# A fused attention and two-layer expert kernel: batch 0 grouped, its TensorE and ScalarE order pinned, weight conversions and softmax steps moved to other slots

## The chip, the cores and the metric

The kernel runs on one core of one Trainium2 chip. The metric is the device time of one execution in microseconds; the number compared is the median over runs. The engines are named as in the profile: PE is TensorE's matmul (PEld its weight loads), DVE is VectorE, ACT is ScalarE, POOL is GpSimd, and SP is the queue that issues all DMA transfers.

## The reference

Three layers stand behind one another. Everything is float32.

```python
# 1. Nystrom attention, batch 8, heads 8, S = 576, D = 64, m = 32 landmarks (means over 18 rows)
A  = softmax(scale * q    @ k_lm.T)      # 576 x 32
Bm = softmax(scale * q_lm @ k_lm.T)      #  32 x 32
C  = softmax(scale * q_lm @ k.T)         #  32 x 576
Z  = Bm.T / (norm1(Bm) * norm_inf(Bm) + 1e-6)
for _ in range(6): Z = 2 * Z - Z @ Bm @ Z
x = A @ Z @ C @ v                        # 4608 tokens x 512 after the heads are joined
# 2. gated layer, width 1536
x = (silu(x @ w_gate) * (x @ w_val)) @ w_out
# 3. soft mixture of 8 experts with 4 slots each
logits = x @ phi                         # 4608 x 32
d = softmax(logits, over the tokens); c = softmax(logits, over the slots)
slot_in = d.T @ x                        # 32 x 512
out = c @ expert_ffn(slot_in)            # relu(s @ w1[e]) @ w2[e]
```

## The kernel before

The attention result is never formed. Per batch b the right-hand factor Z C v is multiplied into the gate and value weights, so that one chunk j of 128 of the 1536 columns needs only the softmaxed scores A (tiles `EH` and `EL`, a high and a low part) times a small matrix G (tiles `GH`, `GL`). The program has three stages.

**The head** (first 40 us). `first_attention` (L361) does the attention of batch 0 alone: landmark sums, scores, softmax and a Newton chain (`m_n`, `m_T`, tile `newton`), and ends with the block `WB`. Pieces of weight conversion are put between its steps (`side`).

**The batches.** For each of 8 batches, `unit` (L948) runs 12 chunks. A chunk has two halves of 288 tokens; a half has six matmuls into a PSUM tile `pg` (gate), an eviction to `u` by ACT (Silu), six matmuls into `pv` (value) and a product `hT` by DVE. After each of these four groups comes a slot, so a batch has 48 slots, n = 4j + i, and the function `slot` puts all other work there by the table `SCHED`:

- `g_product` (L740) multiplies `WB` into the weights: eight matmuls into two PSUM tiles `g`, for one chunk (256 columns) or for a pair of chunks (512 columns); `paired` (L737) decides. ACT then writes `GH`, and DVE subtracts to get `GL` one slot later. Before, batch 0 is never paired.
- `logits` (tile `l`) and `transposes` (into `HB`) of the chunk before.
- `attention(b + 1)` and `a_softmax(b + 1)` (lists `at1`, `at2`, `at3`, `am1` to `am3`; numbers are slots counted from the start of the batch before): landmark sums by DVE (L333), scores `m_a` and `m_c`, exponentials by ACT, the transposes `m_t`, and six Newton steps `m_n` (L670).
- `softmoe(b - 1)` (lists `sm`, `sm1`): softmax of the logits of the batch before, `DN`, an exchange of `DN` between partitions (twelve small DMA transfers, or four matmuls `m_dr` in batch 7), 72 matmuls `m_d` into four PSUM tiles, and their addition to `Sacc` (L921).
- In batch 0 only: the conversion of the weights from float64 storage (lists `w`, `o`: one ACT pass, L176, and for each 512 columns two DVE operations, L192 and L193), and for each chunk the product of `w_out` and phi (list `p`: four transposes `m_wt`, four products `m_p`, one sum `m_ps`, each followed by an ACT copy).

PSUM tiles come from pools by tag: `x` has three buffers (g, m_a, m_c, m_t, m_n, m_d, m_wt, m_p, m_ps), `pg` and `pv` two each, `l` one. A matmul that needs a buffer waits until the engine that evicts the tile from it is done.

**The tail** (last 84 us) loads the expert weights, runs the experts and writes the output.

What sets the order: each engine runs its instructions in one order. From batch 1 on, `keep_order` (L73) pins PE to the order in which the code is written. In the head and in batch 0 the framework's scheduler may reorder the instructions of an engine. Inside SP's queue transfers are issued strictly one after the other, and one that waits for its buffer holds up those behind it. Silu and Exp need different tables in ACT; a change of table is an `ACT_TABLE_LOAD`.

Of the kernel before, what the change touches and what calls it, by code (L numbers as in the profile page):

```python
# [8 lines left out]
F32 = mybir.dt.float32  # L9
# [18 lines left out]
SCHED = {  # L28
# [22 lines left out]
}  # L51
# [3 lines left out]
def nystrom_softmoe_kernel(  # L55
# [488 lines left out]
    def attention(b):  # L544
        assert b == 1 or ("q", b - 1) in seq
        ks, qs = landmark_tiles()
        for nm, dst in (("k", ks), ("q", qs)):
            for hp in range(4):
                (landmark_pool if b == 1 and S_["lp"][2 * hp + (nm == "q")] else landmark)(nm, b, hp, dst)
                if hp == 3 and b > 1:  # L550
                    load_four("q" if nm == "k" else "k", b)
                yield
        def score_tiles(name):
            ms = [psp.tile([128, 512], F32, tag="pv" if i == 3 else "x", name=name, bufs=2 if i == 3 else 3)
                  for i in (3, 0, 1, 2)]
            return {(1, 1): ms[0], (0, 0): ms[1], (0, 1): ms[2], (1, 0): ms[3]}
# [22 lines left out]
        for name, product, eviction in (  # L579
                ("m_a", lambda half, ms: scores(ms, ks, "q", b, half, range(4)), a_eviction),  # L580
                ("m_c", c_product, c_eviction)):
            if together:
                t = score_tiles(name)
                for half in (1, 0):
                    product(half, [t[half, 0], t[half, 1]])
                for half, r in ((1, 1), (0, 0), (0, 1), (1, 0)):
                    eviction(half, r, t[half, r])
                    yield
            else:
                for half in range(2):  # L590
                    ms = [psp.tile([128, 512], F32, tag="x", name=name, bufs=3) for r in range(2)]
                    product(half, ms)
                    for r in range(2):
                        eviction(half, r, ms[r])
                        yield
        if b == 1:
            e_tiles(b)
# [71 lines left out]
        for k in range(6):  # L669
            m = psp.tile([128, 512], F32, tag="x", name="m_n", bufs=3)  # L670
            for q in range(2):
# [65 lines left out]
    def paired(b, j):  # L737
        return 0 < b < nb - 1 and not (b == nb - 2 and j >= NJ - 2)

# [208 lines left out]
    def unit(b, j, slot):  # L948
# [3 lines left out]
        for half in range(2):  # L952
            pg = psp.tile([128, 512], F32, tag="pg", name="pg", bufs=2)
            mm3(pg, b, j, 0, half)
            u = mp.tile([128, HALF], F32, tag="u", name="u", bufs=2)
            by_tanh = 0 < b < nb - 1 and (j, half) in TANH[b > 1]
            if by_tanh:
# [22 lines left out]

    TANH = [{(5, 0), (5, 1), (6, 0)}, {(1, 1), (2, 0), (2, 1)}]
    GROUPS = [2, 2, 4, 8, 8, 8, 4]
# [33 lines left out]

    first_attention(side)
    load_w(5)
    for f in side_pre:
# [67 lines left out]
    for a in range(1, nb):  # L1087
        att, asm = attention(a), a_softmax(a)
        for gen, nm in ((att, "at"), (asm, "am")):
            for r in S_[nm + str(min(a, 3))]:  # L1090
                todo[48 * (a - 1) + r].append(gen)
        sm = softmoe(a - 1)
        for r in S_["sm1" if a == 1 else "sm"]:
            todo[48 * a + r].append(sm)
    prev = None
    n_ins = lambda: len(nc.cur_bb.bb.instructions)
    for b in range(nb):
        if b == 1:
            middle = n_ins()
        for j in range(NJ):  # L1100
            p = prev
            def slot(i):
# [24 lines left out]
                if not first:  # L1127
                    for gen in todo[48 * b + n]:
                        next(gen, None)
                if n == (46 if b == 0 else 45) and b + 1 < nb:  # L1130
                    g_unit(b + 1, 0)
                if n == (47 if b == 0 else 46):
                    g_low()
# [211 lines left out]
```

## Time and profile before

| what | value |
|---|---|
| median of 3 runs | 676.5 us (674.85 to 676.81) |
| the profiled execution | 674.4 us, its span 672.6 us |
[...]
| PE busy | 623.9 us, 93% of the span |
| DVE, ACT, POOL busy | 478.0, 298.8, 73.3 us |
| batches 0 to 7 begin at | 40.4, 125.9, 200.3, 266.2, 332.1, 398.0, 463.9, 527.7 us |
| the last pv matmul ends at | 588.4 us |

The profiled execution lies 2.1 us under the median of the runs. A batch begins here with its first pg matmul. Matmuls overlap, so a busy PE is not a PE at its peak; the difference between a stretch and its busy time is idle time. In rows of stretches each row has its bounds and length in us, the busy time and number of instructions of each engine, and at its end the granted TensorE clock, the busy share of the DMA engines and the GB/s that they moved.

### The profile page before, as it was taken

Reading aid. Unit: us, or ns where it says so; the run is one execution under the profiler, and the core shown is the slowest. Engines: PE = TensorE matmul, PEld = TensorE weight load, DVE = VectorE, ACT = ScalarE, POOL = GpSimd, SP = SyncE. Lnnn points to the kernel's source line nnn. Section 1 sums busy time; section 2 is a strip of 40 time slices with the busy share of each in tenths; the row PEclk is TensorE's granted clock in tenths of the full one; section 3 lists DMA queues with packets and bytes.
Section 4 is the critical chain, followed back from the end, with each engine's and each line's share of the span. In section 5 each row is a group of like instructions: output and inputs, shape, how many; then the busy total and the mean of one; then the engine's idle time right before and its main releaser. Section 6 shows DMA issues by size and latency. Waiting matters only on the chain. (4 is left out here: it accounts for less than half of the span.)

```text
span 672.6 us, 18315 instructions
## 1 busy us (share of the span) xinstructions
PE 623.9 (93%) x7591; PEld 465.8 (69%) x7591; DVE 478.0 (71%) x1154; ACT 298.8 (44%) x764; POOL 73.3 (11%) x81
## 2 busy tenths in 40 slices
PE   5699999998999999999999999999999999989991
PEld 2575667784877877787787778777778777843560
DVE  4999989878578777868785978597856645550441
ACT  2566875445438323732383338233823442320441
POOL 0400012013011101110111012001300000010000
PEclk9799999998999999999999999999999999999996
DMA  8788773233222222222222222122120595699999
GB/s 281 271 322 331 269 280 129 87 113 116 73 72 83 75 72 73 84 75 73 72 86 73 71 87 76 69 71 72 57 86 2 160 378 184 220 288 348 348 369 337
DMA packets 63299, 106.47 MB, mean 158 GB/s; under 512 B 4977, under 2 KB 33009, under 8 KB 61681
## 3 DMA queue, kind: packets, MB, share of 16 engines
q1 hardware_dynamic: 63216, 105.32, 47.1%
q8 instruction: 59, 0.97, 0.6%
q14 instruction: 24, 0.19, 0.1%
HBM read 91.24 MB, written 12.58 MB: 154 GB/s over the span
## 5 line engine op out<-in xcount | busy, mean ns | idle before, releaser
L312 ACT ACTIVATE u<-pg 128x288 f32<-128x288 f32 x174 | 71.9, 413 | 138.4 <-PE pg L945 130.8
L974 DVE TENSOR_TENSOR hT<-u,pv 128x288 f32<-128x288 f32 x174 | 77.7, 447 | 40.1 <-PE pv L945 36.3
L945 PE MATMUL pg<-EH,GH 128*128 128x288 f32 x384 | 93.9, 324 | 2.6 <-ACT GH L765 1.6
L779 DVE TENSOR_TENSOR GL<-g,GH 128x512 fp32r<-128x512 f32 (+1 forms) x122 | 66.4, 572 | 37.7 <-ACT GH L765 37.6
L945 PE MATMUL pg<-EH,GL 128*128 128x288 f32 x384 | 85.7, 299 | 1.7 <-DVE GL L779 1.5
L945 PE MATMUL pv<-EH,GH 128*128 128x288 f32 x384 | 84.0, 298 | 0.0
L945 PE MATMUL pg<-EL,GH 128*128 128x288 f32 x384 | 83.5, 296 | 0.0
L945 PE MATMUL pv<-EL,GH 128*128 128x288 f32 x384 | 82.6, 296 | 0.0
L945 PE MATMUL pv<-EH,GL 128*128 128x288 f32 x384 | 82.2, 295 | 0.0
L765 ACT CAST GH<-g 128x512 fp32r<-128x512 f32 (+1 forms) x122 | 54.2, 495 | 55.0 <-PE g L748 54.9
L945 PEld LDWEIGHTS pg<-EH,GH 128*128 128x128 f32 x384 | 60.0, 189 | 22.8 <-issue 15.5
L799 DVE STREAM_TRANSPOSE HB<-hT 128x576 f32<-128x576 f32 x96 | 74.3, 774 | 1.8
L945 PEld LDWEIGHTS pg<-EH,GL 128*128 128x128 f32 x384 | 62.2, 188 | 4.7 <-DVE GL L779 3.8
L945 PEld LDWEIGHTS pv<-EH,GH 128*128 128x128 f32 x384 | 61.6, 188 | 2.6 <-issue 1.2
L945 PEld LDWEIGHTS pg<-EL,GH 128*128 128x128 f32 x384 | 61.8, 188 | 0.9 <-issue 0.9
L945 PEld LDWEIGHTS pv<-EL,GH 128*128 128x128 f32 x384 | 61.5, 188 | 0.9 <-issue 0.9
L945 PEld LDWEIGHTS pv<-EH,GL 128*128 128x128 f32 x384 | 61.6, 188 | 0.5 <-issue 0.5
L748 PE MATMUL g<-w,WB 64*32 64x512 f32 (+1 forms) x976 | 56.4, 510 | 0.4 <-ACT WB L535 0.4
L794 PE MATMUL l<-hT,P_sb 128*32 128x160 f32 (+1 forms) x768 | 45.2, 298 | 0.8 <-DVE hT L974 0.6
L794 PEld LDWEIGHTS l<-hT,P_sb 128*32 128x32 f32 x768 | 15.2, 108 | 39.8 <-DVE hT L974 16.5
L913 PE MATMUL m_d<-HB,HB 32*32 32x384 f32 x864 | 38.4, 514 | 2.6 <-DMA HB<-DN 2.3
L913 PE MATMUL m_d<-HB,DN 32*32 32x384 f32 x288 | 37.7, 514 | 0.0
(248 smaller groups left out, 946.4 us busy)
## 6 DMA issues: line engine op xcount, KB each, us to landing
k<-in_kT_dram SPq DMA_DIRECT2D x52, 288.0 KB, 3.7
ffn<-in_w_dram SPq DMA_DIRECT2D x13, 1024.0 KB, 9.0
ffn<-in_w_dram SPq DMA_DIRECT2D x24, 512.0 KB, 9.0
HB<-in_w_cat_dram SPq DMA_DIRECT2D x8, 1024.0 KB, 8.0
v<-in_v_dram SPq DMA_DIRECT2D x8, 1024.0 KB, 5.8
q<-in_qT_dram SPq DMA_DIRECT2D x28, 288.0 KB, 3.0
HB<-in_w_out_dram SPq DMA_DIRECT2D x12, 512.0 KB, 5.8
wr<-in_w_cat_dram SPq DMA_DIRECT2D x4, 1024.0 KB, 8.7
```

Of the source, the lines that this page charges most:

```text
L312: i = act.activation(*a, **kw)
L748: pe.matmul(gs[r][32 * hp:32 * hp + 32, 0:256 * n].rearrange("p (u f) -> p u f", u=n), WB[b % 2][64 * r:64 * r + 64, hp, :], w[64 * r:64 * ...
L765: act.copy(H_, g)
L779: dve.tensor_tensor(out=GL, in0=g, in1=GH, op=ALU.subtract)
L794: pe.matmul(L[32 * c:32 * c + 32, 0:32 * k], P_sb[:, j, :], main[:, 0:k, c, :], start=j == 0, stop=j == NJ - 1)
L799: dve.transpose(HB[b % 2][:, S * j:S * j + S].rearrange("p (t r) -> p t r", r=32), hT[:, 0:S].rearrange("p (t r) -> p t r", r=32))
L913: pe.matmul(ms[a][32 * g:32 * g + 32, 0:384].rearrange("p (j f) -> p j f", j=NJ), d_of(a, g, k), hb[32 * a:32 * a + 32, :, 4 * k + g, :], ...
L945: pe.matmul(ps[:, 0:HALF], G_t[b, j, q, sel_][h], e[:, q, ts_], start=n == 0, stop=n == 5)
L974: dve.tensor_tensor(out=o, in0=u, in1=pv[:, 0:HALF], op=ALU.mult)
```

## The change

The core of the diff; of the tables only the lines that are spoken of stand here, and `w`, `o`, `p`, `at1`, `am1`, `at2`, `am2` get new slot numbers throughout.

```diff
-    'loads': ['w1', 'q0', 'o0', 'w0', 'v0', 'o1', 'q1', 'v1', 'w2', 'w4', 'p', 'w3'],
+    'loads': ['w1', 'q0', 'o0', 'w0', 'v0', 'o1', 'q1', 'w2', 'w3', 'w4', 'p', 'v1'],
...
-    'sm1': [1, 2, 4, 19, 20, 21, 24, 25, 25, 28],
+    'sm1': [1, 2, 4, 13, 15, 16, 25, 26, 26, 28],
+    'sm7': [1, 2, 3, 6, 10, 15, 23, 24, 24, 28],
...
-    'u0': [1, 3, 3, 0],
+    'u0': [1, 1, 1, 0],
...
-    'lw': [0, 0, 0, 0, 0, 0, 0, 0, 0, 0, 0, 0],
+    'lw': [0, 0, 0, 0, 0, 1, 0, 1, 0, 1, 0, 1],
...
@@ attention(b): the landmark sums of q come behind the scores m_a for b == 1
+        yield from landmarks("k", ks)
+        if b > 1:
+            yield from landmarks("q", qs)
...
+                if name == "m_a":
+                    yield from landmarks("q", qs)
@@ the Newton steps
-            m = psp.tile([128, 512], F32, tag="x", name="m_n", bufs=3)
+            m = psp.tile([128, 512], F32, tag="pg", name="m_n", bufs=2)
@@
     def paired(b, j):
-        return 0 < b < nb - 1 and not (b == nb - 2 and j >= NJ - 2)
+        return (b > 0 or j >= 4) and b < nb - 1 and not (b == nb - 2 and j >= NJ - 2)
@@ unit
-            by_tanh = 0 < b < nb - 1 and (j, half) in TANH[b > 1]
+            by_tanh = b < nb - 1 and (j, half) in TANH[min(b, 2)]
@@
-    TANH = [{(5, 0), (5, 1), (6, 0)}, {(1, 1), (2, 0), (2, 1)}]
+    TANH = [{(4, 1), (5, 0), (5, 1)}, {(3, 1), (4, 0), (4, 1)}, {(1, 1), (2, 0), (2, 1)}]
@@
     first_attention(side)
+    in_order("silu", warm, one, AF.Silu)
@@ the lists of generators for each slot
+    for a in range(1, nb):
         sm = softmoe(a - 1)
-        for r in S_["sm1" if a == 1 else "sm"]:
+        for r in S_["sm1" if a == 1 else "sm7" if a == nb - 1 else "sm"]:
             todo[48 * a + r].append(sm)
@@
+    middle = n_ins()
     for b in range(nb):
         if b == 1:
-            middle = n_ins()
+            keep_order(mybir.EngineType.Activation, middle, n_ins())
```

So in batch 0 chunks 4 to 11 get their G in pairs; PE's order is pinned from batch 0 on and ACT's within batch 0; four of the weight conversions (chunks 5, 7, 9, 11) do their low word with a second ACT pass, and need two DVE operations fewer each; three halves of batch 0 get their Silu from Tanh, which saves a change of table, at one DVE operation each; the Silu table is loaded in the head; the attention of batches 1 and 2 runs some slots earlier; within a slot the steps of all attention generators come ahead of those of `softmoe`; the Newton steps use the PSUM buffers of `pg`.

**PE in batch 0, around the G product of chunks 4 and 5.** Tiles as above (`HB_85` is the work space of the `w_out` product; in the rows of the changed kernel line numbers are 1 to 7 higher). Before, the unit of chunk 5:

```order
L945 MATMUL pg<-EH,GH 128x288
L945 MATMUL pv<-EH,GH 128x288
L945 MATMUL pg<-EH,GH 128x288
L794 MATMUL l<-hT,P_sb 32x160 x2
L794 MATMUL l<-hT,P_sb 32x128 x2
L945 MATMUL pg<-EL,GH 128x288 x2
L945 MATMUL pg<-EH,GL 128x288
L945 MATMUL pv<-EH,GH 128x288
L269 MATMUL m_wt<-cst,HB_85 128x128 x4
L945 MATMUL pg<-EH,GL 128x288
L945 MATMUL pv<-EL,GH 128x288 x2
L945 MATMUL pv<-EH,GL 128x288 x2
```

Now, from the paired G product in the unit of chunk 3 on:

```order
L755 MATMUL g<-w_630,WB_75 32x512 x8
L801 MATMUL l<-hT,P_sb 32x160 x2
L801 MATMUL l<-hT,P_sb 32x128 x2
L279 MATMUL m_p<-HB_85 32x128 x4
L952 MATMUL pg<-EH,GH 128x288 x2
L952 MATMUL pg<-EL,GH 128x288 x2
L952 MATMUL pg<-EH,GL 128x288 x2
L952 MATMUL pv<-EH,GH 128x288 x2
L952 MATMUL pv<-EL,GH 128x288 x2
L952 MATMUL pv<-EH,GL 128x288 x2
L285 MATMUL m_ps<-cst,HB_85 128x32
L270 MATMUL m_wt<-cst,HB_85 128x128 x4
```

The groups of six matmuls stay whole, the other work stands between them, and one G product of 512 columns serves two chunks.

**PE in batch 2, where `softmoe` and the Newton steps meet** (the same in batches 3 to 6). Before, the end of m_d and what follows it:

```order
L913 MATMUL m_d<-HB_85,DN 32x384
L913 MATMUL m_d<-HB_85,HB_84 32x384 x2
L672 MATMUL m_n<-RV,bd 128x96 x2
L945 MATMUL pg<-EH,GH 128x288 x2
L945 MATMUL pg<-EL,GH 128x288 x2
```

Now, the beginning of m_d and what stands ahead of it:

```order
L801 MATMUL l<-hT,P_sb 32x160 x2
L801 MATMUL l<-hT,P_sb 32x128 x2
L679 MATMUL m_n<-RV,bd 128x96 x2
L920 MATMUL m_d<-HB_85,DN 32x384
L920 MATMUL m_d<-HB_85,HB_84 32x384 x4
```

The Newton step moved from behind the m_d matmuls to the place ahead of them.

**ACT in batch 0, at the exponentials of batch 1's attention** (`CE`, `AN` its score tiles; `w_...` a weight conversion, `HB_85<-HB_85` one of `w_out`). Before, its first change of table and the change back:

```order
L312 ACT_TABLE_LOAD
L312 ACTIVATE CE_617,stat<-CE_617,stat 128x576
L176 ACTIVATE HB_85<-HB_85 128x512
L765 CAST GH<-g 128x256 x2
L285 COPY P_sb<-m_ps 128x32
L312 ACTIVATE CE_617,stat<-CE_617,stat 128x32
L312 ACTIVATE CE_618,stat<-CE_618,stat 128x576
L312 ACTIVATE CE_618,stat<-CE_618,stat 128x32
L176 ACTIVATE HB_85<-HB_85 128x512
L312 ACT_TABLE_LOAD
L312 ACTIVATE u<-pg 128x288
```

Now, the only change of table to Exp in batch 0 and what follows it:

```order
L313 ACT_TABLE_LOAD
L313 ACTIVATE CE_533,stat<-CE_533,stat 128x576
L313 ACTIVATE CE_533,stat<-CE_533,stat 128x32
L286 COPY P_sb<-m_ps 128x32
L271 COPY HB_85<-m_wt 128x512
L313 ACTIVATE CE_534,stat<-CE_534,stat 128x576
L313 ACTIVATE CE_534,stat<-CE_534,stat 128x32
L313 ACTIVATE AN_530<-AN_530 128x576
L313 ACTIVATE AN_531<-AN_531 128x576
L966 ACTIVATE u<-pg 128x288
L177 ACTIVATE w_953<-HB_85 128x1024
```

The four exponentials share one table load, and the eviction `u` behind them is a Tanh (L966) and needs no other table.

## Rows read from the trace of the kernel before

**Rows 1.** Batches 0, 1, 3, 7, tail: length; PE, PEld, DVE, ACT, POOL busy (count).
```profile
40.38:125.93 85.55, 81.79 (x931) 60.02 (x930) 78.78 (x182) 59.90 (x141) 8.75 (x7) 1.00 0.72 262
125.93:200.28 74.35, 70.78 (x862) 53.21 (x859) 54.86 (x131) 31.50 (x82) 10.59 (x10) 0.98 0.28 86
266.17:332.08 65.91, 64.80 (x826) 51.01 (x825) 51.78 (x127) 29.06 (x77) 8.45 (x8) 1.00 0.25 77
527.74:588.41 60.67, 58.35 (x714) 45.87 (x712) 33.37 (x75) 21.65 (x57) 0.12 (x1) 1.00 0.78 261
588.41:672.60 84.19, 65.04 (x724) 35.02 (x723) 28.62 (x80) 24.19 (x58) 4.71 (x11) 0.93 1.03 337
```

**Rows 2.** What PE waited for in batch 0: total us, times, longest.
```profile
PE pg L945 <- ACT GH L765: 1.6, 2, 0.9
PE pg L945 <- ACT u L312: 0.9, 1, 0.9
```

**Rows 3.** Batches 0 and 3, tile pg: length; PE, PEld, DVE, ACT busy.
```profile
40.38:125.93 85.55, 29.48 (x144) 20.99 (x144) 0.00 (x0) 9.95 (x24) 1.00 0.72 262
266.17:332.08 65.91, 24.71 (x144) 20.32 (x145) 1.35 (x3) 9.90 (x24) 1.00 0.25 77
```

**Rows 4.** The same stretches, tile pv: length; PE, PEld, DVE busy.
```profile
40.38:125.93 85.55, 26.66 (x144) 20.84 (x144) 10.43 (x24) 1.00 0.72 262
266.17:332.08 65.91, 22.98 (x146) 20.46 (x144) 10.62 (x24) 1.00 0.25 77
```

**Rows 5.** The same stretches, tile g (columns as in rows 3).
```profile
40.38:125.93 85.55, 9.42 (x192) 2.55 (x192) 9.92 (x25) 8.32 (x25) 1.00 0.72 262
266.17:332.08 65.91, 6.53 (x96) 1.09 (x96) 7.97 (x13) 6.42 (x12) 1.00 0.25 77
```

**Rows 6.** Timeline of PE, batch 1: start, us, instruction, idle before and releaser.
```profile
157.07 0.83 PE L913 MATMUL m_d<-HB,DN 32*32 32x384 f32 x2
...
161.87 0.51 PE L913 MATMUL m_d<-HB,HB 32*32 32x384 f32 x2 [2.28 <-DMA HB<-DN]
...
167.56 0.53 PE L945 MATMUL pv<-EH,GH 128*128 128x288 f32 x2
```

**Rows 7.** Timeline of SP, batch 1: the exchange of DN.
```profile
152.77 7.81 SPq L879 DMA_DIRECT2D HB<-DN  x12
```

**Rows 8.** A stretch within batch 1's m_d (columns as in rows 1).
```profile
162.86:166.27 3.41, 3.41 (x84) 2.41 (x92) 2.86 (x5) 0.00 (x0) 1.49 (x2) 0.50 0.45 138
```

**Rows 9.** Timeline of PE, batch 3: the first m_d and the Newton step.
```profile
299.56 0.51 PE L913 MATMUL m_d<-HB,DN 32*32 32x384 f32 x1
...
304.53 0.69 PE L672 MATMUL m_n<-RV,bd 128*128 128x96 f32 x4 [0.65 <-DVE Sacc L923]
```

**Rows 10.** Timeline of PE, batch 7: the exchange by matmuls.
```profile
538.53 0.55 PE L882 MATMUL m_dr<-DN,cst 32*128 32x160 f32 x6 [1.92 <-DVE DN L867]
```

**Rows 11.** DVE in batch 0, groups: shapes, count, busy us, mean ns, idle before.
```profile
L974 DVE TENSOR_TENSOR hT<-u,pv 128x288 f32<-128x288 f32 x24 | 10.7, 447 | 2.2 <-PE pv L945 1.7 <-ACT u L312 0.6
L192 DVE TENSOR_SCALAR w<-w 128x512 int32<-128x512 int32 x20 | 10.0, 522 | 0.5 <-ACT w L176 0.3
L779 DVE TENSOR_TENSOR GL<-g,GH 128x256 fp32r<-128x256 f32 x24 | 9.2, 416 | 0.5 <-ACT GH L765 0.5
L333 DVE TENSOR_REDUCE qs<-q 128x32 f32<-128x576 f32 x4 | 2.9, 741 | 0.0
```

**Rows 12.** ACT in batch 0, groups: table loads and one conversion pass.
```profile
L176 ACT ACTIVATE w<-HB 128x1024 f32<-128x1024 f32 x6 | 6.9, 1147 | 0.0
L312 ACT ACT_TABLE_LOAD x5 | 6.4, 1283 | 0.9 <-DVE stat L608 0.9
```

**Rows 13.** Timeline of ACT in the head: a copy of the Newton chain.
```profile
26.07 0.27 ACT L503 COPY newton<-m_n 128x128 f32<-128x128 f32 x1 [1.00 <-PE m_n L468]
```

**Rows 14.** Timeline of SP in the head: the load of batch 1's v.
```profile
34.71 0.38 SPq L165 DMA_DIRECT2D v<-in_v_dram  x1
```

**Rows 15.** Page, DMA issues: KB each, median us to landing.
```profile
wr<-in_w_cat_dram SPq DMA_DIRECT2D x4, 1024.0 KB, 8.7
```

More of the change, by code (lines that the diff above doesn't have):

```diff
@@ L546, in attention, with landmarks @@
         ks, qs = landmark_tiles()
-        for nm, dst in (("k", ks), ("q", qs)):
+        def landmarks(nm, dst):
             for hp in range(4):
-                (landmark_pool if b == 1 and S_["lp"][2 * hp + (nm == "q")] else landmark)(nm, b, hp, dst)
+                landmark(nm, b, hp, dst)
                 if hp == 3 and b > 1:
@@ L1129, in slot @@
                         next(gen, None)
-                if n == (46 if b == 0 else 45) and b + 1 < nb:
+                if n == 45 and b + 1 < nb:
                     g_unit(b + 1, 0)
-                if n == (47 if b == 0 else 46):
+                if n == 46:
                     g_low()
```

18 rows, old and new, of the table SCHED are left out of this document.

## The prediction

> **What bounds the kernel now.** The first view is the busy time by stretch [rows 1]. In a middle batch TensorE is busy 64.80 of 65.91 us and the vector engine only 51.78, so TensorE is the bound there, with 1.11 us idle. Batch 0 is 85.55 us long, 19.64 longer, and has two engines near their limit: TensorE 81.79 and DVE 78.78. ACT has 59.90. Batch 1 takes 74.35, which is 8.44 above a middle batch. In the tail the DMA share is 1.03 at 337 GB/s with PE busy 65.04 of 84.19: the transfers bound it. Its loads go into space that the work before it sets free, so I count a gain ahead of the tail in full, and come back to that for batch 7.
>
> Then I asked what TensorE waits for in batch 0. The waits over half a microsecond are two on `GH` (1.6 together) and one on `u` (0.9) [rows 2], most of the idle time of 85.55 - 81.79 = 3.76 us. Next the same busy time by tile. The 144 pg matmuls take 29.48 in batch 0 and 24.71 in batch 3 [rows 3], about as many pv matmuls 26.66 and 22.98 [rows 4]: the same work is 4.77 + 3.68 = 8.45 us dearer. The order of before shows why that can be: the scheduler puts other work into the middle of a group of six. The G product takes 9.42 against 6.53 [rows 5].
>
> Then the timelines at the two places where batches 1 and 7 differ from a middle batch. In batch 1 the `m_d` stretch goes from 157.07 to 167.56, 10.49 us, with a wait of 2.28 on the exchange of `DN` in it [rows 6]; the twelve transfers are issued from 152.77 on for 7.81 us [rows 7], so the last landed 161.87 - 152.77 = 9.1 us after the first issue. Behind that wait the granted clock is 0.50 for 3.41 us, although PE is busy in all of them [rows 8]. The same matmuls in batch 3 take 299.56 to 304.53, 4.97 us, and the Newton step behind them waits 0.65 on the addition to `Sacc`, which has to free its PSUM buffer [rows 9]. In batch 7 `m_dr` waits 1.92 on `DN` [rows 10].
>
> **The change part by part.** The sum is made against the profiled execution, 674.4 us, which is 2.1 under the median of the runs.
>
> Batch 0, the G product. In before, 192 matmuls take 9.42: the eleven single products (chunks 1 to 11) and one pair for batch 1. With a pair at 6.53 / 6 = 1.088, a single one is (9.42 - 1.09) / 11 = 0.757 [rows 5]. Eight singles become four pairs: 8 x 0.757 - 4 x 1.088 = 1.70 saved on TensorE.
>
> Batch 0, the idle time. With pairs `GH` is needed four times less often, and the groups of six stay whole, so an eviction has more matmuls before it is asked for. Nothing says that each wait goes. I take half of 3.76, 1.9; bounds 0 and 3.76.
>
> Batch 0, the pinned order. If switching between tiles makes the 8.45 dearer, pinning gives some of it back; part of it may be DVE and ACT sharing PSUM in a crowded batch, and that stays. No row separates these. I take a quarter, 2.1; bounds 0 and 8.45.
>
> What limits these three is DVE. Removed there: eight conversion operations of 0.522 (four chunks, two each), 4.18; sixteen `GL` subtractions of 0.416 become eight of twice the size, which I price at 0.613 from the paired batch (7.97 for 13 instructions [rows 5]): 6.66 - 4.90 = 1.75. Added: three Tanh halves with one operation like `hT`, 3 x 0.447 = 1.34, and three more landmark sums, 3 x 0.741 = 2.22 [rows 11]. That is 78.78 - 5.93 + 3.56 = 76.4, so batch 0 cannot fall by more than 85.55 - 76.4 = 9.2, however well TensorE does. My sum for batch 0 is 1.70 + 1.9 + 2.1 = 5.7, which leaves it at 79.9 us with DVE 96% busy. Its other bound is a loss of 3, below.
>
> ACT in batch 0 loses three of five table loads (3.85; one of the other two moves into the head) and gains four conversion passes of 1.147 [rows 12], 4.6: about even, at 60 of 80 us. I give no gain for the tables themselves. Rows 2 show PE waiting 2.5 us on ACT in all, and that is already in the idle term. [...]
>
> Batch 1. `DN` now comes out at slot 15, the exchange goes out at slot 16, and `m_d` begins at slot 25. Nine slots at about 67.0 / 48 = 1.40 us are 12.6 us (67.0 is a batch 1 without its excess but with the 1.1 us of a second `m_a` pass), against the 9.1 that the exchange needs [rows 6, 7]; 3.5 us to spare. Then the wait and the half clock behind it are gone and `m_d` takes what it takes in batch 3: 10.49 - 4.97 = 5.5 [rows 6, 9]. What may delay the exchange are the transfers ahead of it on SP's queue, above all the loads of k and q, which move with the landmarks. Bounds: 0 if all of it stays, and 8.44 - 1.1 = 7.3 at the other end.
>
> Batches 2 to 6. The Newton step goes ahead of `m_d` and to the buffers of pg, so it no longer waits for `Sacc`: 5 x 0.65 = 3.3 [rows 9]. Its cost is a pg buffer that must be free. There are two, and a pg tile is read by ACT some 0.41 us (9.90 / 24 [rows 3]) while six pv matmuls run for about 0.96 (22.98 / 24 [rows 4]); so it is free by then, and I take nothing. Bounds: 0, if the same wait shows up at the next user of an `x` buffer, to 3.7, if half a microsecond more of the idle 5.5 (5 x 1.11) goes with it.
>
> Batch 7. `DN` at slot 10 and `m_dr` at 15 put five slots (some 6 us) where the wait was 1.92 [rows 10]: 1.9 saved. The low bound is 0: here the DMA share is already 0.78 [rows 1] and a batch that ends sooner may only meet its loads sooner. The high one is 2.3, all the idle 60.67 - 58.35.
>
> The head. A Silu table load of 1.283 [rows 12] now stands on ACT before a copy of the Newton chain that had an idle 1.00 ahead of it [rows 13]; what does not fit is at least 0.3, and more with the small activation that calls for it and the new order around it. I take 0.6; bounds 0 and 1.5. The load of batch 1's `v`, which went out at 34.71 [rows 14] ahead of four weight loads, now goes last. That lets weights arrive earlier, and helps batch 0's start; I count it at nothing, hidden in TensorE's backlog, and if it were not hidden it would be on the good side.
>
> Sum: -5.7 - 5.5 - 3.3 - 1.9 + 0.6 = -15.8, and 674.4 - 15.8 = 658.6 for an execution like the profiled one. The median lies a little above it; with about 1 us, **659.5 us**.
>
> **The rivals.** A: batch 0 gives its gain back. ACT, pinned, runs strictly in the written order, and the weight conversions stand in it: one that waits for its transfer or for DVE holds the `GH` and `u` evictions behind it. The load of chunk 7's weights goes out at the end of slot 11's conversion and is used at slot 16, five slots of 85.55 / 48 = 1.78, 8.9 us, and these loads take 8.7 at the median [rows 15]. For it: no spare time, DVE at 96%. Against it: a load that goes out as the conversion's buffer comes free has been early in most chunks, and ACT has 20 us to spare. Batch 0 is then as long as before or up to 3 longer (three late conversions of 1 us); with 1.5, 674.4 + 1.5 - 5.5 - 3.3 - 1.9 + 0.6 = 665.8, median **667**. [...]
>
> B: the earlier exchange does not help. If the twelve transfers stand behind loads on SP's queue that wait for their buffers, `m_d` waits as before, and the change does not do there what it is written for: 658.6 + 5.5 = 664.1, median **665**. For it: the queue is strictly in order. Against it: in batch 1 the DMA share is 0.28 [rows 1], and the slack is 3.5 us.
>
> C: slower. The m_d case shows the price of a long wait: 2.28 us idle brought 3.41 us at half clock, 5.5 together [rows 6, 8]. If the pinned batch 0 had three such waits on ACT or DVE, it would lose 16.5 and gain nothing: 674.4 + 16.5 - 5.5 - 3.3 - 1.9 + 0.6 = 680.8, median **682**. It decides from two on: the gains elsewhere are 10.1 and two stalls cost 11. Against it: the longest wait of batch 0 is now 0.9 [rows 2], and DVE, which would have to be late, has less to do.
>
> **How the numbers follow.** The forecast 0.72; A 0.16; B 0.06; C 0.06. The likeliest is 659.5. Its own terms go from -9.2 - 7.3 - 3.7 - 2.3 = -22.5 to about -8 (A's and B's sums); all at their best end together is unlikely, so the range goes from 650 to 670: it takes in A and B with some microseconds to spare, and leaves C out. A measurement of this kernel can tell some 0.3%, 2 us, from no change. Faster by more than that 0.91; within it 0.03, A with batch 0 worse than its bound; slower 0.06, C.
>
> **What would show it.** Right: batch 0 at about 80 us, its pg matmuls near 27 to 28 us, DVE at 76 in it, no wait over 1 us; in batch 1 no wait on `DN` ahead of `m_d`, clock 1.00 there, length 67 to 69; batches 2 to 6 at 65.2 with no wait on `Sacc`; batch 7 near 58.7; the first pg matmul within 41.9. Wrong: batch 0 above 85 with waits on ACT (A); the exchange landing after slot 25 (B); stretches at a clock of 0.5 in batch 0 (C); or a tail that grows by what the batches lose, because its loads and not TensorE set the end.

## The result and the profile after

The changed kernel takes 668.56 us at the median of 4 runs (667.78 to 669.73), the kernel before 675.67 (674.61 to 676.81): a ratio of 0.9896, interval 0.9871 to 0.9921. It is faster, by 7.1 us where 15.8 were forecast; 668.56 lies in the range on record but far above 659.5, and nearest to rival A's 667. The span of the profiled execution went from 672.58 to 666.63.

Where the time went, from the first pg matmul of each batch and the last pv matmul:

| stretch | before | after | measured | forecast |
|---|---|---|---|---|
| head | 40.38 | 40.33 | -0.05 | +0.6 |
| batch 0 | 85.55 | 89.10 | +3.55 | -5.7 |
| batch 1 | 74.35 | 67.20 | -7.15 | -5.5 |
| batches 2 to 6 | 327.46 | 323.94 | -3.52 | -3.3 |
| batch 7 | 60.67 | 58.09 | -2.58 | -1.9 |
| tail | 84.17 | 87.97 | +3.80 | 0 |

The stretches of the changed kernel, in the columns of [rows 1] (batches 0, 1, 3, 7, tail):

```profile
40.33:129.43 89.10, 76.75 (x869) 61.53 (x869) 76.39 (x172) 59.70 (x135) 8.74 (x7) 0.96 0.64 220
129.43:196.63 67.20, 66.34 (x860) 51.63 (x858) 51.48 (x129) 30.95 (x81) 10.54 (x10) 1.00 0.31 93
261.76:326.92 65.16, 64.96 (x827) 51.13 (x826) 51.24 (x127) 29.39 (x77) 8.30 (x8) 1.00 0.25 78
520.57:578.66 58.09, 57.69 (x714) 45.62 (x712) 33.09 (x75) 21.45 (x57) 0.12 (x1) 1.00 0.80 272
578.66:666.60 87.94, 66.64 (x724) 35.80 (x723) 28.67 (x80) 24.18 (x58) 4.75 (x11) 0.92 0.98 323
```

Batches 1 to 7 do what was forecast and more. Batch 0 is the riddle: PE has 5.04 us less to do than before (76.75 against 81.79 in [rows 1]) and yet the batch is longer, so PE's idle time (length less busy time) rose from 3.76 to 12.35. The waits of PE in batch 0 answer to [rows 2]:

```profile
PE m_wt L270 <- DVE HB L194: 10.4, 10, 3.4
PE m_ps L285 <- ACT HB L280: 1.7, 1, 1.7
PE pg L952 <- ACT GH L772: 0.5, 1, 0.5
PE m_n L679 <- DVE RV L695: 0.2, 1, 0.2
```

The old waits on `GH` and `u` are down to 0.5; a new one is there ten times, `m_wt` on the last DVE step of the `w_out` conversion. The same batch for the tiles pg, pv and g, in the columns of [rows 3 to 5]:

```profile
40.33:129.43 89.10, 26.02 (x145) 20.63 (x145) 1.33 (x3) 9.93 (x24) 0.96 0.64 220
40.33:129.43 89.10, 22.95 (x144) 20.43 (x144) 10.29 (x23) 0.96 0.64 220
40.33:129.43 89.10, 8.28 (x128) 1.71 (x128) 9.36 (x18) 7.53 (x17) 0.96 0.64 220
```

The pg and pv matmuls got cheaper by 3.46 and 3.71 us, 7.2 of the 8.45. Not all of that is saved, since matmuls of different tiles overlap: PE's busy time in the whole batch fell by the 5.04 above, and the G product's by 1.14 (8.28 against 9.42). The longest of the new waits stands in the unit of chunk 5. PE's timeline there, with the idle time before each row and its releaser:

```profile
81.05 0.41 PE L285 MATMUL m_ps<-cst,HB 128*128 128x32 f32 x2 [1.65 <-ACT HB L280]
84.87 1.11 PE L270 MATMUL m_wt<-cst,HB 128*128 128x128 f32 x4 [3.42 <-DVE HB L194]
```

ACT's timeline ahead of it:

```profile
73.31 1.28 ACT L313 ACT_TABLE_LOAD   x1
...
77.31 1.25 ACT L313 ACTIVATE AN<-AN 128x576 f32<-128x576 f32 x2
78.46 0.39 ACT L966 ACTIVATE u<-pg 128x288 f32<-128x288 f32 x1
78.75 1.12 ACT L177 ACTIVATE w<-HB 128x1024 f32<-128x1024 f32 x1
79.77 1.06 ACT L772 CAST GH<-g 128x512 fp32r<-128x512 f32 x2
80.71 0.28 ACT L280 COPY HB<-m_p 128x128 f32<-128x128 f32 x1
80.87 0.71 ACT L177 ACTIVATE HB<-HB 128x512 f32<-128x512 f32 x1
```

DVE's timeline behind it:

```profile
81.59 0.63 DVE L786 TENSOR_TENSOR GL<-g,GH 128x512 fp32r<-128x512 f32 x1
82.13 1.12 DVE L193 TENSOR_SCALAR HB<-HB 128x512 int32<-128x512 int32 x1
83.17 0.68 DVE L786 TENSOR_TENSOR GL<-g,GH 128x512 fp32r<-128x512 f32 x1
83.77 0.44 DVE L967 SCALAR_TENSOR_TENSOR u<-u,pg 128x288 f32<-128x288 f32 x1
84.13 0.68 DVE L194 SCALAR_TENSOR_TENSOR HB<-HB 128x512 int32<-128x512 int32 x1
```

Read backward: `m_wt` waits for the DVE step of 84.13; DVE's first step (82.13) could not begin before ACT's conversion pass of 80.87 was through at 81.58, and DVE put other work ahead of each of its two steps; that pass stood on ACT behind the table load and the four exponentials, which now stand together from 73.31 to 78.5, and behind what had gathered after them. PE, in written order, had nothing else to do. Within the second wait, at 82.24, the granted clock fell to 0.50; the second row is a stretch of the tail:

```profile
82.24:89.07 6.83, 4.20 (x19) 4.13 (x20) 6.83 (x16) 3.12 (x10) 2.14 (x2) 0.50 0.44 145
590.83:594.24 3.41, 3.35 (x14) 2.25 (x16) 1.90 (x4) 0.00 (x0) 2.49 (x2) 0.50 0.60 166
```

In the tail PE stops within `m_d` for a reason that no other engine gives ("issue"). Its timeline:

```profile
587.60 0.48 PE L920 MATMUL m_d<-HB,DN 32*32 32x384 f32 x1
590.04 0.83 PE L920 MATMUL m_d<-HB,HB 32*32 32x384 f32 x4 [1.97 <-issue]
590.80 0.90 PE L814 MATMUL warm<-cst 128*128 128x160 f32 x2
```

The DMA queues (packets, MB, share) show what that is. From 579.5 to 587.6 only the data queue moved, nearly without a gap:

```profile
q1 hardware_dynamic: 1468, 2.52, 95.8%
```

The load of PE's next instructions came behind that, at 587.74 (the window from 587.6 to 589). That queue 8 carries PE's is an estimate: the changed kernel's page has 2 x 7527 matmuls and weight loads and 59 packets, 255 for each packet.

```profile
q1 hardware_dynamic: 491, 0.49, 99.3%
q8 instruction: 1, 0.02, 4.2%
```

The load before it had come at 569.45. In the kernel before, one went through at 583.44, 5 us ahead of the last pv matmul, where the data left room (579.5 to 588.4):

```profile
q1 hardware_dynamic: 594, 1.17, 45.1%
q8 instruction: 1, 0.02, 0.7%
```

So 1.97 us without instructions and, as an estimate from 3.35 us of work at half clock, some 1.7 us lost there make nearly all of the tail's 3.8; the first matmul of the experts (`m_f`) begins 3.69 us later behind the last pv matmul, 22.10 us against 18.41.

### The profile page after: what moved, and what is told of

The parts are those of the page before. It is cut to its first block, busy times and chain, and to the rows that moved or that the text cites. A ratio compares the mean times of both kernels' runs of the same rounds, so it can differ in the third digit from the quotient of the medians.

```text
span 666.6 us, 18185 instructions
## 1 busy us (share of the span) xinstructions
PE 616.1 (92%) x7527; PEld 467.6 (70%) x7527; DVE 468.5 (70%) x1141; ACT 300.9 (45%) x759; POOL 72.9 (11%) x81
## 5 line engine op out<-in xcount | busy, mean ns | idle before, releaser
L786 DVE TENSOR_TENSOR GL<-g,GH 128x512 fp32r<-128x512 f32 (+1 forms) x114 | 64.7, 597 | 38.5 <-ACT GH L772 38.4
L952 PE MATMUL pv<-EH,GH 128*128 128x288 f32 x384 | 82.0, 295 | 0.0
L801 PEld LDWEIGHTS l<-hT,P_sb 128*32 128x32 f32 x768 | 15.1, 108 | 43.6 <-DVE hT L981 15.8
L920 PE MATMUL m_d<-HB,HB 32*32 32x384 f32 x864 | 36.0, 491 | 2.0 <-issue 2.0
L920 PE MATMUL m_d<-HB,DN 32*32 32x384 f32 x288 | 35.1, 491 | 0.0
```

The source lines that it names most:

```text
L786: dve.tensor_tensor(out=GL, in0=g, in1=GH, op=ALU.subtract)
L801: pe.matmul(L[32 * c:32 * c + 32, 0:32 * k], P_sb[:, j, :], main[:, 0:k, c, :], start=j == 0, stop=j == NJ - 1)
L920: pe.matmul(ms[a][32 * g:32 * g + 32, 0:384].rearrange("p (j f) -> p j f", j=NJ), d_of(a, g, k), hb[32 * a:32 * a + 32, :, 4 * k + g, :], ...
L952: pe.matmul(ps[:, 0:HALF], G_t[b, j, q, sel_][h], e[:, q, ts_], start=n == 0, stop=n == 5)
```

## The experiments

All times of the kernel before in these runs lie at 674.7 to 675.2 us at the median. Batch and tail lengths come from each run's trace, which is of one execution; those of e1 (666.58 us) and e11 (661.06) lie 2.0 above and 3.2 below their medians. Three runs whose edits lie outside batch 0 (e3, e7, e8) have 88.65 to 89.00 us there against 89.10, so half a microsecond says nothing. In e1 and e15 the granted clock also fell within the head, from 33.32 to 36.7, and batch 0 began at 42.20 and 42.39, in the other runs at 39.1 to 41.1; for these two its end is given too.

**e1_transposes_later.** The `w_out` product two slots later.

```diff
-    'p': [[-1, 2, 2], [3, 2, 2], [7, 2, 2], [11, 2, 2], [15, 2, 2], [19, 2, 2], [23, 2, 2], [27, 2, 2], [31, 2, 2], [35, 2, 2], [39, 2, 2], [43, 2, 2]],
+    'p': [[-1, 2, 2], [5, 2, 1], [9, 2, 1], [13, 2, 1], [17, 2, 1], [21, 2, 1], [25, 2, 1], [29, 2, 1], [33, 2, 1], [37, 2, 1], [41, 2, 1], [45, 1, 1]],
```

> Changed kernel with the w_out product of each chunk (m_wt, m_p, m_ps) two slots later, so that three slots instead of one lie between the last DVE step of its conversion and the m_wt transposes. Theory 1 (PE's pinned order puts m_wt too close behind DVE): the ten waits of m_wt on DVE (10.4 us) and the half clock behind them go, batch 0 falls from 89.1 to 77 to 80 us, the whole to 657 to 660 us. Rival 1 (DVE is behind as a whole in batch 0, the wait only moves to another matmul): batch 0 stays above 86, the whole above 665.

664.60 us, ratio 0.9841 (0.9802 to 0.9880); batch 0 85.00, its end 2.2 us earlier than in the changed kernel (127.20 against 129.43). The waits of `m_wt` are gone, as theory 1 says, but half of its gain does not come: PE's idle time fell by 7.5 us, to 4.82, while its busy time rose by 3.4, to 80.18. Waits of PE in batch 0, PE and ACT at the longest one:

```profile
PE m_ps L285 <- ACT HB L280: 2.3, 1, 2.3
PE l L801 <- ACT P_sb L286: 1.0, 2, 0.8
```

```profile
77.97 0.64 PE L285 MATMUL m_ps<-cst,HB 128*128 128x32 f32 x2 [2.28 <-ACT HB L280]
```

```profile
75.30 1.28 ACT L313 ACT_TABLE_LOAD   x1
76.59 0.78 ACT L313 ACTIVATE CE<-CE,stat 128x576 f32<-128x576 f32 x1
...
77.67 0.24 ACT L280 COPY HB<-m_p 128x128 f32<-128x128 f32 x1
```

The copy that `m_ps` needs stands behind the table load and the first exponentials, a wait of 2.28 us where it had been 1.65, and the granted clock is 0.50 from 77.70 to 84.52, with PE busy in 6.55 of these 6.82 us. The G product takes 10.54 us here against 8.28; why is not shown. PE waited these 2.28 us for a copy of 0.24 us that stood behind work PE does not need.

**e2_batch0_unpinned** and **e4_act_unpinned.** The scheduler's order back in batch 0, for PE and ACT, or for ACT alone.

```diff
         if b == 1:
-            keep_order(mybir.EngineType.Activation, middle, n_ins())
+            middle = n_ins()
```

```diff
         if b == 1:
-            keep_order(mybir.EngineType.Activation, middle, n_ins())
+            pass
```

> Changed kernel with PE's and ACT's order pinned only from batch 1 on, all tables as changed. Theory 1: the scheduler puts other matmuls ahead of an m_wt that is not ready, most of the 10.4 us of waits go, but pg and pv get dearer again by some microseconds as in the kernel before; batch 0 80 to 85 us, the whole 660 to 665. Rival 2 (the new slots themselves, not the pinned order, make batch 0 long): batch 0 stays within 2 us of 89.1, the whole at 667 to 671.

668.86 us, ratio 0.9898 (0.9859 to 0.9937); batch 0 88.82. Rival 2 has it: with the scheduler's freedom `m_wt` still waits 4.8 us in two places and pg and pv get dearer again (28.82 and 25.76), so the new slots make batch 0 as long unpinned as pinned.

> Changed kernel with PE pinned in batch 0 as changed but ACT's order there left to the scheduler. Theory 1: ACT's order is not what costs, the waits of m_wt on DVE stay at about 10 us and the whole lies within 2 us of 668.6. Rival A of the prediction (evictions on ACT held up behind conversions): batch 0 falls by 3 us or more, the whole to 665 or less.

662.89 us, ratio 0.9817 (0.9779 to 0.9854); batch 0 85.78, waits of `m_wt` 3.5. Here rival A's forecast comes true and theory 1 falls in part: ACT's fixed order costs 3.3 us of batch 0. The whole fell by 5.7, since the tail is shorter too, 85.42, with a wait for instructions of 0.7 us. Against e2, PE's fixed order alone is worth 3.0 us of batch 0.

**e3_fill_in_head.** 56 tiny matmuls where PE waits in the head.

```diff
+        mw = psp.tile([128, 512], F32, tag="l", name="fill")
+        for _ in range(56):
+            pe.matmul(mw[0:32, 0:32], cst[:, 0:32], cst[:, 0:32], start=True, stop=True)
         mn = psp.tile([128, 512], F32, tag="l", name="m_nx")
```

> Changed kernel with 56 more tiny matmuls (32x32) on PE in the head, in a wait of 5.3 us, so that PE's instruction loads fall some 110 instructions earlier in the program. Theory 3 (the tail is 3.75 us longer because one PE instruction load stood behind the expert weights' transfers, 1.97 us idle and half clock behind it): that load now goes out ahead of the weights, the tail falls from 87.9 to about 84.2 and the whole from 668.6 to about 665. Rival 3 (the loads of the expert weights set the end of the tail): the tail stays at 87 to 88 and the whole at 668 to 670.

665.82 us, ratio 0.9861 (0.9830 to 0.9891). The wait for instructions is gone, `m_f` begins 18.74 us after the last pv matmul, against 22.10 in the changed kernel and 18.41 before. But a load still comes at 587.99, behind the data, and not ahead of it as theory 3 says; PE only does not run out of instructions by then. The tail is 86.06: 1.5 us of the gain are lost again in its last part, behind `m_f`, and why is not shown.

**e5_later_act_free.** The edits of e1 and e4 together.

> The w_out product two slots later (as in the run before with that edit) and, beside it, ACT's order in batch 0 left to the scheduler. Theory 1b (two waits in a row make batch 0 long: m_wt close behind DVE, and, once that is gone, m_ps behind the copy of m_p that stands on ACT behind the grouped exponentials; each of 2 us or more is followed by half clock): the 2.3 us wait of m_ps and the half clock behind it go, batch 0 falls from 85.0 to 78 to 80 us, the whole to 656 to 660. Rival 1b (DVE with 76 us of work is the bound as it stands): batch 0 stays at 83 or above, the whole at 662 or above.

667.27 us, ratio 0.9888 (0.9858 to 0.9917); batch 0 87.90. Theory 1b falls, and rival 1b's numbers hold: PE's waits now have seven causes (2.2 on DVE's transposes of `m_a`, 2.2 on `P_sb`, 2.0 on the copy of `m_p`, 1.6 on `RV`), so leaving ACT's order to the scheduler, which gained 3.3 us with the changed slots, loses 2.9 with the later ones.

**e6_newton_in_x.**

```diff
-            m = psp.tile([128, 512], F32, tag="pg", name="m_n", bufs=2)
+            m = psp.tile([128, 512], F32, tag="x", name="m_n", bufs=3)
```

> Changed kernel with the Newton steps m_n back in the three x buffers, their place ahead of m_d kept. Theory (the new order alone removes the wait on Sacc): batches 2 to 6 stay within 0.2 us of 65.13. Rival (the pg buffers remove it): batches 2 to 6 return to 65.7 or more, with a wait of 0.5 us or more on Sacc each.

677.64 us in one run; batches 2 to 5 take 66.27 to 66.34, longer than before the change (65.89 to 65.91), and batch 1 takes 69.48. Waits of PE from batch 2 to 6:

```profile
PE m_d L920 <- DVE RV L695: 2.2, 5, 0.4
```

The rival's length comes true, with another wait than its own: ahead of `m_d` the Newton step holds an x buffer that `m_d` needs, 0.4 of the 1.15 us a batch. The order alone loses 0.4 us a batch against the kernel before; with the pg buffers it gains 0.75.

**e7_sm1_old** and **e8_sm7_old.**

```diff
-    'sm1': [1, 2, 4, 13, 15, 16, 25, 26, 26, 28],
+    'sm1': [1, 2, 4, 19, 20, 21, 25, 26, 26, 28],
```

```diff
-        for r in S_["sm1" if a == 1 else "sm7" if a == nb - 1 else "sm"]:
+        for r in S_["sm1" if a == 1 else "sm"]:
```

> Changed kernel with DN of batch 1 back at slot 19 and the exchange at slots 20 and 21, m_d still from slot 25 on. Theory (the early exchange is what shortens batch 1): 5 slots are 7 us against the 9.1 that the exchange needs, so m_d waits about 2 us on DN again and runs at half clock behind it; batch 1 goes from 67.2 to 71 to 74 us. Rival (other parts, the batch 0 work no longer running over into batch 1, shorten it): batch 1 stays below 69.

677.64 us in one run; batch 1 75.19. PE's wait there, and SP's queue with the exchange:

```profile
PE m_d L920 <- DMA HB<-DN: 4.3, 1, 4.3
```

```profile
158.74 3.82 SPq L886 DMA_DIRECT2D HB<-DN  x5
162.66 0.53 SPq L166 DMA_DIRECT2D v<-in_v_dram  x1
163.23 0.51 SPq L167 DMA_DIRECT2D v<-in_v_dram  x1
163.79 2.49 SPq L886 DMA_DIRECT2D HB<-DN  x4
```

Without the early exchange batch 1 is 7.99 us longer, and 0.84 longer than before the change: here the load of `v` stands in the middle of the exchange, the wait is 4.3 where it was 2.28 in [rows 6], and half clock holds for 6.83 us. So the theory is right that the early exchange is what shortens batch 1; the 7.99 holds the new place of `v` too.

> Changed kernel with batch 7 on the common list sm instead of sm7. Theory (DN five slots ahead of m_dr removes its wait): the wait of 1.9 us of m_dr returns and batch 7 goes from 58.1 to 60 to 60.7 us; the tail keeps its 88 us, so the whole gets 2 us longer. Rival (the loads of batch 7 and the tail take back what batch 7 gains): the tail gets shorter by as much, the whole stays within 0.5 us.

671.24 us in one run; batch 7 62.18 with the wait of 1.9 and 3.41 us of half clock behind it, which the kernel before did not have behind the same wait; the tail 87.14. So `sm7` is worth 4.1 us in the batch here, and 2.7 of the whole. Whether the tail takes back 0.8 is not shown: tails with a wait of 1.6 us or more for instructions lie between 87.1 and 89.4.

**e10_p_on_4j.** Between the changed kernel and e1.

```diff
-    'p': [[-1, 2, 2], [3, 2, 2], [7, 2, 2], [11, 2, 2], [15, 2, 2], [19, 2, 2], [23, 2, 2], [27, 2, 2], [31, 2, 2], [35, 2, 2], [39, 2, 2], [43, 2, 2]],
+    'p': [[-1, 2, 2], [4, 2, 2], [8, 2, 2], [12, 2, 2], [16, 2, 2], [20, 2, 2], [24, 2, 2], [28, 2, 2], [32, 2, 2], [36, 2, 2], [40, 2, 2], [44, 2, 1]],
```

> Changed kernel with the w_out product one slot later (m_wt at slot 4j, m_p at 4j + 2, m_ps at 4j + 4), so that the copy of m_p stands on ACT ahead of the grouped exponentials, PE and ACT pinned as changed. Theory 1c (the long waits and the half clock behind them are what batch 0 lost): m_wt waits 3 us or less in all, no wait of 2 us, no half clock, batch 0 from 89.1 to 79 to 82 us, the whole to 658 to 662. Rival 1b (DVE is behind as a whole): PE waits in many small pieces in their place, batch 0 at 84 to 88, the whole at 663 to 668.

664.80 us, ratio 0.9836 (0.9804 to 0.9868); batch 0 85.22. Both lengths lie where rival 1b has them, but not for its reason: `m_wt` waits 0.4 in all, as theory 1c says, and in the unit of chunk 5 PE still stops at one piece, now `g` for 2.4 us on the `P_sb` copy behind the exponentials, with 3.41 us of half clock behind it.

**e11_low_words_on_act.** e10 with the fill of e3 and the low words of six more conversions on ACT.

```diff
-    'lw': [0, 0, 0, 0, 0, 1, 0, 1, 0, 1, 0, 1],
+    'lw': [0, 0, 1, 1, 1, 1, 1, 1, 1, 1, 1, 1],
```

> The run before (w_out product on slots 4j) with the low word of six more weight conversions done by an ACT pass, so that DVE has about 5.4 us less to do in batch 0 and ACT about 7 us more, and with the 56 tiny matmuls in the head that move PE's instruction loads. Rival 1b (DVE is the bound of batch 0): batch 0 becomes 3 to 5 us shorter than in the run before. Theory 1c (only the order matters): batch 0 stays within 1 us of the run before, or gets longer by ACT's longer queue. Theory 3 on the tail: no wait for instructions, m_f begins 18 to 19 us after the last pv matmul, the tail at 84 to 86.5 us.

664.21 us, ratio 0.9843 (0.9808 to 0.9878); batch 0 86.50 with DVE at 73.14 and ACT at 65.08. Three microseconds off DVE, with six more on ACT, gained nothing: batch 0 is 1.3 us longer than in e10 and ends 0.5 earlier. The tail is 84.31, `m_f` begins at 18.42, no wait for instructions.

**e12_dve_relieved.**

```diff
+            fs = f32_bits(raw[kind, j], dst[0], n, low_by_act)
+            if kind == "w" and j >= 2:
+                fs = fs[:1] + [lambda: None] * (len(fs) - 1) if low_by_act else [lambda: None] * len(fs)
-            todo_.extend(f32_bits(raw[kind, j], dst[0], n, low_by_act))
+            todo_.extend(fs)
```

> Changed kernel with the DVE steps of the weight conversions of chunks 2 to 11 left out (their weights lose their low words and their right scale), about 19 us of the 76 us of DVE's work in batch 0; order and slots as changed. Rival 1b (the m_wt waits come from DVE being behind): the waits of m_wt fall from 10.4 to under 3 us and batch 0 to 80 us or less. Theory 1 (one slot is too short a distance for DVE's step, whatever else DVE does): the waits stay above 6 us and batch 0 above 85.

664.95 us in one run; batch 0 84.99. PE's wait in it:

```profile
PE m_wt L273 <- DVE HB L194: 6.8, 9, 1.6
```

With DVE busy 61.88 of 84.99 us `m_wt` still waits nine times, 0.75 on average, so two thirds of the new wait stay, as theory 1 has it, and a third went with DVE's load. Batch 0 is at theory 1's bound of 85 and not above it: 4.1 us shorter, with 3.41 us of half clock in place of 6.83.

**e13_batch0_unpaired.**

```diff
-        return (b > 0 or j >= 4) and b < nb - 1 and not (b == nb - 2 and j >= NJ - 2)
+        return 0 < b < nb - 1 and not (b == nb - 2 and j >= NJ - 2)
```

> Changed kernel with batch 0's G products single again. Prediction's term (pairing saves 1.70 us of PE and 1.75 us of DVE): batch 0 gets 1.7 us longer, about 90.8. Rival (PE waits for DVE there, so PE's time for g is not what counts, DVE's is): it gets longer by more, 2.5 to 4 us, in further waits of m_wt; or, if neither counts, it stays within 0.7 us of 89.1.

666.26 us in one run; batch 0 89.33, 0.2 longer, batch 1 67.93, 0.7 longer. Pairing is worth almost nothing in batch 0 while PE waits for others, and about 1 us with batch 1: PE's busy time rose by 1.43 in batch 0, its idle time fell by 1.20. The tail is 84.06, without a wait for instructions: the single products change the number of PE's instructions too.

**e14_exps_spread, e15_spread_dve_relieved, e16_spread_fill.** e10 with the exponentials apart; that with e12's edit; that with e3's.

```diff
-    'at1': [0, 0, 1, 2, 3, 4, 7, 8, 8, 9, 9, 10, 11, 12, 15, 16, 16, 18, 18, 19, 20, 21, 23, 23, 23, 24, 27, 29, 31, 33, 35, 37, 39, 43],
-    'am1': [11, 12, 13, 13, 19, 19, 21, 22, 23, 24, 26, 28, 30, 31, 32, 33, 36],
+    'at1': [0, 0, 1, 2, 3, 4, 7, 8, 8, 9, 9, 10, 11, 12, 15, 16, 16, 17, 17, 19, 20, 21, 23, 23, 23, 24, 27, 29, 31, 33, 35, 37, 39, 43],
+    'am1': [11, 12, 13, 13, 21, 22, 23, 23, 24, 24, 26, 28, 30, 31, 32, 33, 36],
```

> The w_out product on slots 4j and the four exponentials of batch 1's attention no longer in one block on ACT but with the evictions between them (exponentials at slots 17, 19, 21 and 22). Theory 1d (the block of 4.8 us on ACT holds up m_ps's copy and with it the PSUM buffer that g waits for): the wait of 2.4 us of g and the 3.4 us at half clock behind it go, chunk 5 falls from 11.9 us to 8 or 9, batch 0 from 85.2 to 81 to 82 us. Rival 1b (DVE's load): another wait takes the place, batch 0 stays at 84 or above.

665.57 us, ratio 0.9850 (0.9822 to 0.9878); batch 0 85.31. Theory 1d falls: another wait takes the place, as the rival says.

```profile
PE m_ps L285 <- ACT HB L280: 2.3, 1, 2.3
PE l L801 <- ACT P_sb L286: 1.0, 2, 0.6
```

The table load and one pair of exponentials, 2.4 us, now stand ahead of the copy of `m_p`. Batch 0 in the columns of [rows 1]:

```profile
40.75:126.06 85.31, 79.58 (x868) 59.05 (x869) 75.41 (x172) 59.04 (x135) 8.50 (x7) 0.98 0.66 228
```

> The run before with the DVE steps of the weight conversions of chunks 2 to 11 left out (low words and right scale of those weights missing), 15 us less for DVE. Theory 1d: what is left is PE's own work, batch 0 falls by less than 2 us against the run before. Rival 1b: DVE holds batch 0 wherever ACT does not, and batch 0 falls by 3 us or more, to 76 to 79 us.

663.17 us in one run. Batch 0, in the columns of [rows 1]:

```profile
42.39:124.31 81.92, 76.53 (x869) 58.00 (x869) 61.77 (x140) 59.17 (x135) 8.09 (x7) 1.00 0.67 236
```

3.4 us less than e14, its end 1.75 us earlier. That is rival 1b's gain, but not by its mechanism, and 81.9 is above its 76 to 79: PE's idle time hardly fell, from 5.73 to 5.39, with the same wait of 2.3 us of `m_ps` in it. What fell is PE's busy time, by 3.05; e14 has 3.41 us of half clock in batch 0 and e15 none, and e15's batch began 1.64 us later. So these two runs do not show that DVE's load holds the rest.

> The run with the exponentials spread, and the 56 tiny matmuls in the head that move PE's instruction loads. Theories 1d and 3 together: batch 0 at 81 to 82 us, the tail at 84 to 86.5 us without a wait for instructions, the whole at 656 to 661, faster than both kernels. Rivals: batch 0 at 84 or above, or a tail of 87.5 or more with a wait for instructions; the whole at 663 or above.

661.95 us (660.16 to 662.11), ratio 0.9784 (0.9757 to 0.9811): clearly faster than both kernels, through the later slots of the `w_out` product and the tail and not through the exponentials; batch 0 misses the forecast 81 to 82. Batch 0 and the tail:

```profile
40.43:125.76 85.33, 79.52 (x868) 59.06 (x869) 75.38 (x173) 59.00 (x135) 8.50 (x7) 0.98 0.68 233
574.94:660.27 85.33, 65.02 (x723) 34.97 (x723) 28.61 (x80) 24.18 (x58) 4.71 (x11) 0.92 1.01 333
```

## Why the prediction was right and wrong

**Batch 0 is the step that failed**, and in it the term "the idle time": the prediction took the waits that the trace showed, 3.76 us, and asked how many would go. It gave no price to the new slots of `o` and `p`, which put `m_wt` one slot behind its conversion where there had been three. Where 1.9 us of idle time were to go, 8.6 came: 12.35, with 10.4 us of waits of `m_wt`, which PE in its pinned order can't leave; nor does the scheduler's freedom make the batch shorter (e2). The exponentials, which the text counted as even on ACT by their sum, became a block that holds up what stands behind it. The other two terms were too small together: PE's busy time fell by 5.04 us where 1.70 + 2.1 = 3.8 were forecast, though 4.20 us of it ran at half clock; the pairs gave 1.14 of PE's time and 0.2 us of the batch (e13). So the miss of 9.25 us is 10.5 of idle time less 1.2 of busy time. What makes the matmuls dear stays open: no run separates the switching between tiles from the sharing of PSUM by DVE and ACT, which the text also named and no run shows, and with PE pinned pv takes 22.95 in the changed kernel, as in batch 3 (22.98), but 25.72 in e14.

What each cause holds the runs bound but do not divide: later slots of the `w_out` product take 3.9 to 4.1 us off the batch (e1, e10), ACT's free order 3.3 (e4), DVE's steps left out 4.1 (e12), and the first two together only 1.2 (e5). With the later slots e14 still lies 5.5 us above the forecast 79.9: 3.9 of it is idle time (5.73 where 1.86 were left to it, most of it waits on ACT), 1.6 busy time, with 3.41 us at half clock. What order would end these waits is open. DVE's whole work, 76.4 by the prediction, was 76.39; as a floor it said too little, since it is an average over a batch, and a wait is made in one slot.

**Rival A had the mechanism, not the object.** It held that a conversion on the pinned ACT would wait for its transfer. No instruction of ACT waited for a transfer in batch 0. What waited was the conversion behind exponentials, and a copy of 0.3 us; e4 shows that ACT's order costs 3.3 us. The batch's loss of 3.55 is just over rival A's bound of 3. **Rival C's** price, half clock behind a long wait, came true once in batch 0: 6.83 us at 0.50, from within the second of two waits, 1.65 and 3.42 us, with PE busy in 4.20 of them.

**Batch 1**: the mechanism was right, the size 1.65 us short. The excess over a middle batch fell from 8.44 to 2.07, close to the bound of 7.3 that the text had. **Batches 2 to 6**: -3.52 against -3.3; e6 adds that the buffers and the place earn it together only. **Batch 7**: -2.58 against -1.9, just over the bound of 2.3; `m_dr` waits 0.4 us. By e8, one run, the list is worth 4.1 us of the batch. **The head** cost nothing.

**The tail** is the second step that failed: "I count a gain ahead of the tail in full". The text did name a tail that takes back what the batches gain, but gave expert loads as the cause. It was one load of PE's instructions behind them. The twelve kernels with the changed kernel's number of PE instructions all wait for instructions there, eleven of them 1.6 to 2.3 us and e4 0.7; the four with another number (e3, e11, e13, e16) do not, and their `m_f` begins 18.41 to 18.74 us after the last pv matmul, as before (18.41). That the tail's last part, from `m_f` to the end, takes 63.7 to 67.3 us in these runs is open.

Added up: batch 0 missed by 9.25 us and the tail by 3.8; the other stretches gave 3.2 more than forecast. That the measured time still lies in the range owes something to luck: the tail's loss was in none of its terms, and most of it was offset by these 3.2.

## What to carry to other kernels

When an order is pinned, don't ask only which of the waits in the trace will go: list, for each instruction that moves, how many slots lie between it and the work that it reads. Here one slot was too short and was paid with 10.4 us of waits of `m_wt`, three slots had none (e1), and the scheduler's freedom did not make up for it either (e2, batch 0 88.82 against 89.10). The four exponentials, grouped to save table loads, stood as one block on ACT (73.31 to 78.5); of such a block, see what stands behind it and who waits for that, not what the engine's sum says. A wait that is removed may be followed by the next one (here `m_wt`, 10.4 us, then `m_ps`, 2.3 in e1, or `g`, 2.4 in e10), so a fix of one is judged by the length of the stretch.

## What the runs showed of the hardware

The load of PE's instructions stood among the packets of the data. Its packets are 16 KB each: 59 of them, 0.97 MB, on queue 8 of the changed kernel's page, and 60 in the three runs with 56 more matmuls (e3, e11, e16). In the tail none came for 18 us (569.45 to 587.74), in the last 8 of which the data queue took 95.8%, and PE stood 1.97 us without work, then ran 3.41 us at half clock.

56 matmuls that compute nothing that is used, put in an idle place 570 us earlier, made the kernel faster (e16 against e14, on one chip: 661.95 and 665.57 us, with ratios to the kernel before whose intervals lie apart). They did not make the load in the tail earlier: it came 9.4 us behind the last pv matmul in e16, at 584.34, and 9.3 in e14, at 584.65, among as much data (e16, 583.9 to 585.5):

```profile
q1 hardware_dynamic: 541, 0.54, 96.5%
q8 instruction: 1, 0.02, 3.8%
```

What differs is that PE has not run out when the load comes. As 56 more matmuls stand ahead in the program, its borders between two loads fall on other instructions; that this is why is an estimate from 60 packets against 59, not measured.

Half clock did not follow each wait of a kind: in e14 a wait of 2.26 us was followed by 3.41 us at 0.50, in e15 one of 2.27 by none; in batch 7 the wait of 1.92 on `DN` was followed by none before [rows 10] and by 3.41 us in e8; in e4 one of 2.40 by none and one of 1.73 by 3.41 us. So half clock behind each wait of 2 us or more, as e5's theory has it, does not hold.
